# Top-k attention and two MLPs on one core: another cost model for the recorded order, decode's high words in PSUM, and zero products on TensorE

## The chip, the cores and the metric

One core of one Trainium2 chip runs the whole program. The time is the device time of one execution in microseconds, lower is better. Five engines work side by side, each on its own list of instructions: PE (TensorE: products; its weight loads are PEld), DVE (VectorE), ACT (ScalarE), POOL (GpSimd) and SP, which here issues almost all DMA transfers, those that transpose among them. TensorE's clock is granted at one of two levels, 1.2 and 2.4 GHz.

## The reference

Attention keeps the 32 largest scores of each row, and its output goes through two MLPs, which the kernel treats as 18 tiles of 128 tokens:

```python
scores = scale * np.matmul(q, k.transpose(0, 1, 3, 2))       # batch 4, 8 heads, 576 x 576, head size 64
kth = np.partition(scores, -top_k, axis=-1)[..., -top_k:-top_k + 1]
scores = np.where(scores >= kth, scores, -1000000000.0)
attn = softmax(scores)                                         # written out in the reference
x = attn @ v                                                   # as 2304 x 512
h = x @ w_in;  g = where(h >= 1, h, where(h <= -1, 0, (h + 1) ** 2 / 4));  x = g @ w_out     # 512 -> 2048 -> 512
h = max(x @ w_in2, 0);  out = (h * h) @ w_out2
```

## The kernel before

**The work.** 144 slots of attention (18 token tiles T of 8 heads) each take four products into the PSUM tile `both` on PE (`scores`; eight half-height ones in the two tiles that straddle a batch), four MAX8 and three MATCH_REPLACE8 on DVE (`topk_ops`, names `m8`, `W`), three passes on ACT with small ones on POOL between them (`nb` is the bias that `exp_bias` makes), a high and a low half `pc` of the probabilities in 16 bits, a DMA transpose `pT`, and 14 products into `acc` (`attend`). The MLPs run as 144 groups, each a quarter of one tile in one MLP: twelve products into an `h` tile of PSUM (`mlp_in`, from `T_x` or `T_y`, which are transposed activations), the activation on ACT and DVE, high and low halves `g` on ACT and POOL, a DMA transpose `gT`, and twelve products into `o` (`mlp_out`). All products of the MLPs are of 512 columns.

**The weights.** The four matrices come as 64-bit floats in two 32-bit words. For a chunk, `w_decode` (L496) lets ACT shape the high words in place (in `wall`, in SBUF), POOL shape the low words into the chunk's place, and DVE join the two with one SCALAR_TENSOR_TENSOR. There are 62 whole chunks and four half ones. `w_norm` adds four small products of each whole chunk to a running sum of its matrix, the PSUM tile `gram`; from the finished sum comes a scale (through a product named `all_`), and `w_split` (L569) makes high and low 16-bit halves of each chunk, some of them through a PSUM tile `lo_`.

**PSUM.** The ring `ps_h` has two buffers, which serve the `h` tiles, the `lo_` tiles and the `all_` products in turn. `gram` and `o` have two buffers of their own in `ps_o`.

**The order.** Nothing is issued while the program is written down. The class `Book` records each operation (`note`, L194), gives it a cost by hand-written rules (`costs`, L261), and `order` (L291) plays a list scheduler through them: on each engine the ready operation with the smallest key goes first, keys being steps of a plan, and the planned starts set the order in which `emit` (L382) hands everything to the engines. Each engine then works through its own list strictly in that order and waits by semaphores for what it really needs. A transfer is planned to land 0.3 us after its share of the wire (L356). The planner takes DVE and POOL as independent.

Of the kernel before, what the change touches and what calls it, by code (L numbers as in the profile page):

```python
# [7 lines left out]
F16 = mybir.dt.float16  # L8
F32 = mybir.dt.float32
I32 = mybir.dt.int32  # L10
U16 = mybir.dt.uint16
BF16 = mybir.dt.bfloat16
AF = mybir.ActivationFunctionType
ALU = mybir.AluOpType
AX = mybir.AxisListType

P = 128
# [28 lines left out]
    half=((15, 150, 158), (14, 161, 168)), wn=1, ws_i1=45, ws_o1=80, ws_i2=113, ws_o2=183, sp_i1=55, sp_o1=87,  # L46
# [13 lines left out]
class View:  # L60


    __slots__ = ("tile", "ap", "how")
# [78 lines left out]


class Op:
    __slots__ = ("n", "engine", "fn", "args", "kwargs", "deps", "succ", "tiles", "new", "cost", "key", "ready", "start", "missing", "load", "move", "banks")


class Book:
# [36 lines left out]
    def note(self, engine, method, fn, args, kwargs):  # L185
        op = Op()
# [18 lines left out]
        for v in ins:  # L205
            c = v.cover()
# [4 lines left out]
        for v in outs:  # L211
            c = v.cover()
            t = v.tile
# [30 lines left out]
        deps.discard(op.n)  # L244
        op.deps = deps
        op.banks = set()
        for v in views:
            if v.tile.ring.psum and v.tile.name in ("both", "acc"):
                c = v.cover()
                op.banks.update((v.tile.name, b) for b in range(c[2] // 2048, (c[3] - 1) // 2048 + 1))  # L250
# [45 lines left out]
    def order(self):  # L296
# [9 lines left out]
        free = dict.fromkeys(engines, 0.0)  # L306
# [2 lines left out]
        now = {e: [] for e in engines}  # L309
        wire = 0.0  # L310
        out = []
        banks = {}

        def ask(op):
            while op.new:
# [13 lines left out]
        while len(out) < len(ops):  # L329
            best = None  # L330
            for e in engines:
                if now[e]:
                    t = free[e]
                elif soon[e]:
                    t = max(free[e], soon[e][0][0])
# [6 lines left out]
            t, e = best  # L342
            while soon[e] and soon[e][0][0] <= t:
                op = ops[heapq.heappop(soon[e])[1]]
                heapq.heappush(now[e], (op.key, op.n))
            op = ops[heapq.heappop(now[e])[1]]
# [3 lines left out]
                continue  # L350
            op.start = t
            busy, took = op.cost
            free[e] = t + busy
            if e == "SP":
                wire = max(wire, t + 1.6) + took
                end = wire + 0.3  # L356
            else:
                end = t + took
            for b in op.banks:
# [42 lines left out]
def tile_topk_attention_mlp_mlp(  # L402
# [42 lines left out]
    ident = cpool.tile([P, P], BF16, tag="ident", name="ident")  # L445
    ones = cpool.tile([P, P], BF16, tag="ones", name="ones")
    neg = cpool.tile([P, P], F16, tag="neg", name="neg")

    def square_norm(src, acc, junk):
        ACT.activation(junk, src, AF.Square, accum_out=acc)  # L450
# [65 lines left out]
    def w_decode(name, c, *half):  # L516
        d = wall[:, W[name]["at"] + c + 1, :].bitcast(I32)
        if half:
            d = d[:, 256 * half[0] : 256 * half[0] + 256]
        words = lambda: raw[(name, c, *half)].rearrange("p (n w) -> p n w", w=2)  # L520
        halves = lambda: raw[(name, c, *half)].bitcast(U16).rearrange("p (n w) -> p n w", w=4)
        hi = lambda: words()[:, :, 1]


        low = lambda: halves()[:, :, 1]
        return [
            lambda: ACT.activation(hi(), hi(), AF.Prelu, scale=2.0**-112, alpha=-(2.0**32)),
            lambda: POOL.tensor_scalar(d, low(), 2.0**-13, 2.0**-14 - 0.5, op0=ALU.mult, op1=ALU.add),
            lambda: DVE.scalar_tensor_tensor(d, hi().bitcast(I32), 3, d, op0=ALU.logical_shift_left, op1=ALU.bitwise_or),
        ]  # L530

    gram = {}
# [17 lines left out]
    def make_ident():  # L550
        t = wall[:, 0, 0:P].bitcast(I32)
        POOL.iota(t, pattern=[[1, P]], base=0, channel_multiplier=-1)
        POOL.memset(ones, 1.0)
        DVE.tensor_scalar(ident, t, 0.0, None, op0=ALU.is_equal)
        DVE.tensor_scalar(neg, ident, -1.0, None, op0=ALU.mult)

# [9 lines left out]
        return diags[name, at]  # L566


    def w_split(name, c):  # L569
        src = wall[:, W[name]["at"] + c + 1, :]  # L570
        hi, lo = w_hi(name, c, 0, 512), w_lo(name, c, 0, 512)
        s = W[name]["s"]
# [504 lines left out]
    def mlp_in(n, fb):  # L1077
        m, T, j = group(n)
        w = "i1" if m == 1 else "i2"
        src = xT[T] if m == 1 else yT[T]  # L1080
        if fb == 0:
            hps[n] = ps_h.tile([P, 4, P], F32, tag="h", name=f"h_{n}")
        h = hps[n].rearrange("p a b -> p (a b)")
        c = 4 * j + fb
        PE.matmul(h, src[:, 0, fb, :], w_hi(w, c, 0, 512), start=(fb == 0), stop=False)
        PE.matmul(h, src[:, 0, fb, :], w_lo(w, c, 0, 512), start=False, stop=False)
        PE.matmul(h, src[:, 1, fb, :], w_hi(w, c, 0, 512), start=False, stop=(fb == 3))

# [241 lines left out]
    first = {}  # L1330
# [93 lines left out]
```

## Time and profile before

| | us |
|---|---|
| median of 3 runs (lowest, highest) | 1129.77 (1126.63, 1132.04) |
| the profiled execution | 1128.01 |
| its span, first to last instruction | 1126.2 |
| PE busy / DVE busy / ACT busy / POOL busy in the span | 989.6 / 910.6 / 865.6 / 718.5 |

The span is the profiled execution without 1.8 us that lie around it. Every time below is of that one execution. Nearly all instructions are recorded by one line, so rows are told apart by tile and shape. "Idle" is the time that an engine stood still just before an instruction, with what released it. PEclk is the mean granted TensorE clock of a stretch as a share of 2.4 GHz; its records begin at 71 us, and before that the column shows 1.00.

### The profile page before, as it was taken

Reading aid. Unit: us, or ns where it says so; the run is one execution under the profiler, and the core shown is the slowest. Engines: PE = TensorE matmul, PEld = TensorE weight load, DVE = VectorE, ACT = ScalarE, POOL = GpSimd, SP = SyncE. Lnnn points to the kernel's source line nnn. Section 1 sums busy time; section 2 is a strip of 40 time slices with the busy share of each in tenths; the row PEclk is TensorE's granted clock in tenths of the full one; section 3 lists DMA queues with packets and bytes.
Section 4 is the critical chain, followed back from the end, with each engine's and each line's share of the span. In section 5 each row is a group of like instructions: output and inputs, shape, how many; then the busy total and the mean of one; then the engine's idle time right before and its main releaser. Section 6 shows DMA issues by size and latency. Waiting matters only on the chain.

```text
span 1126.2 us, 20691 instructions
## 1 busy us (share of the span) xinstructions
PE 989.6 (88%) x6676; PEld 482.4 (43%) x6676; DVE 910.6 (81%) x1967; ACT 865.6 (77%) x1605; POOL 718.5 (64%) x1182
## 2 busy tenths in 40 slices
PE   1257667689998989999999999999999999999997
PEld 1133333334444434444444544444444444444443
DVE  5988887788898887999899989999899999981100
ACT  4769788999867776888789888988778887776542
POOL 4696889989675645566786746567775656453221
PEclk9999788889999999999999999999999999999999
DMA  8987997686895656778987676879767676665332
GB/s 227 319 270 171 269 213 175 135 163 121 166 168 121 114 112 108 150 128 160 157 167 147 121 129 122 156 130 182 152 126 130 114 132 115 112 109 87 67 64 56
DMA packets 463389, 165.22 MB, mean 147 GB/s; under 512 B 441776, under 2 KB 448944, under 8 KB 463280
## 3 DMA queue, kind: packets, MB, share of 16 engines
q1 hardware_dynamic: 459856, 163.05, 71.5%
q10 hardware_dynamic: 3424, 0.85, 0.5%
q8 instruction: 52, 0.85, 0.3%
q14 instruction: 57, 0.47, 0.1%
HBM read 55.31 MB, written 4.72 MB: 53 GB/s over the span
## 4 chain that ended last, share of the span: by engine, by line
PE 38%; DMA 7%; issue 5%; POOL 5%; DVE 5%; ACT 4%; SPq 0%; POOLq 0%; ACTq 0%; DVEq 0%
PE o L385 17%; PE h L385 16%; DMA gT<-g 4%; PE both L385 3%; DVE m L385 2%; PE acc L385 2%; DVE W L385 2%; POOL pc L385 2%; POOL g L385 2%; ACT W L385 1%; DMA T_x<-hl_x 1%; DMA qT<-qhl 1%; ACT r L385 1%; POOL nb L385 1%; DVE r L385 1%
## 5 line engine op out<-in xcount | busy, mean ns | idle before, releaser
L385 PE MATMUL o<-wall,gT 128*128 128x512 f16 x1728 | 430.1, 387 | 19.4 <-DMA gT<-g 19.3
L385 DVE MAX8 m<-W 128x8 f32<-128x576 f32 x432 | 324.3, 755 | 7.1
L385 POOL TENSOR_TENSOR g<-r,g 128x512 f16<-128x512 f32 x144 | 167.6, 1164 | 165.0 <-ACT g L385 145.1
L385 POOL TENSOR_TENSOR pc<-W,pc 128x64 f16<-128x64 f32 (+1 forms) x288 | 207.2, 741 | 102.8 <-ACT pc L385 95.9
L385 PEld LDWEIGHTS <-gT 128*128 128x128 f16 x1728 | 167.3, 99 | 228.4 <-DMA gT<-g 30.1
L385 DVE MATCH_REPLACE8 W<-m,W 128x576 f32<-128x576 f32 x288 | 213.6, 742 | 0.0
L385 PE MATMUL h<-wall,T_x 128*128 128x512 f16 x864 | 208.8, 382 | 4.2 <-DVE r L385 2.1
L385 PE MATMUL h<-wall,T_y 128*128 128x512 f16 x864 | 209.6, 379 | 1.9 <-ACT r L385 1.8
L385 ACT ACTIVATE W<-both,nb 128x576 f32<-128x576 f32 x144 | 106.5, 740 | 86.1 <-POOL nb L385 43.0
L385 DVE MAX8 m<-both 128x8 f32<-128x576 f32 x144 | 108.7, 757 | 48.0 <-PE both L385 40.3
L385 ACT ACTIVATE W<-W,nb,esc 128x576 f32<-128x576 f32 x144 | 124.5, 864 | 8.5 <-POOL nb L385 4.4
L385 PEld LDWEIGHTS <-T_x 128*128 128x128 f16 x864 | 81.2, 98 | 100.4 <-issue 10.0
L385 PEld LDWEIGHTS <-T_y 128*128 128x128 f16 x864 | 80.9, 98 | 92.3 <-ACT r L385 1.7
L385 PE MATMUL both<-kst,qT 128*128 128x64 f16 (+3 forms) x640 | 101.8, 300 | 20.8 <-ACT W L385 20.1
L385 PEld LDWEIGHTS <-pT 128*128 128x128 f16 (+1 forms) x2240 | 92.7, 103 | 55.8 <-issue 24.7
L385 DVE MATCH_REPLACE8 W<-m,both 128x576 f32<-128x576 f32 x144 | 107.5, 747 | 0.0
L385 PE MATMUL acc<-vst,pT 128*128 128x65 f16 (+1 forms) x2240 | 101.1, 197 | 5.7 <-DVE x L385 3.3
L385 ACT ACTIVATE g<-r 128x512 f16<-128x512 f32 x144 | 90.3, 627 | 13.9 <-DVE r L385 12.3
L385 ACT ACTIVATE pc<-W 128x576 f16<-128x576 f32 x144 | 97.7, 679 | 1.5
L385 ACT ACTIVATE r<-r 128x512 f32<-128x512 f32 x144 | 90.4, 628 | 2.0
L385 DVE SCALAR_TENSOR_TENSOR r<-h,G,r 128x512 f32<-128x512 f32 x72 | 53.2, 739 | 36.4 <-ACT h L385 33.7
L385 ACT ACTIVATE r<-h 128x512 f32<-128x512 f32 x72 | 42.5, 590 | 51.9 <-PE h L385 50.5
(143 smaller groups left out, 1102.8 us busy)
## 6 DMA issues: line engine op xcount, KB each, us to landing
wall<-in_moe_w_in_dram SPq DMA_DIRECT2D x32, 512.0 KB, 7.8
wall<-in_moe_w_out_dram SPq DMA_DIRECT2D x30, 512.0 KB, 6.2
out_dram<-ob SPq DMA_DIRECT2D x18, 256.0 KB, 2.3
l_q<-in_q_dram SPq DMA_DIRECT2D x16, 256.0 KB, 3.5
n_v<-in_v_dram SPq DMA_DIRECT2D x24, 144.0 KB, 2.9
n_k<-in_k_dram SPq DMA_DIRECT2D x12, 288.0 KB, 3.2
l_k<-in_k_dram SPq DMA_DIRECT2D x12, 288.0 KB, 3.4
pT<-pc SPq DMA_TRANSPOSE x144, 3.4
```

Source lines behind the costliest of these rows:

```text
L385: op.fn(*(real(a) for a in op.args), **{k: real(a) for k, a in op.kwargs.items()})
```

## The change

1. **The planner's costs.** An operation of DVE with two inputs in SBUF of more than 64 elements (`port`) and any operation of POOL are planned as excluding each other. The landing of a transposing transfer is planned 1.6 us later than before (`LATE`).
2. **The decode.** POOL's step comes first; ACT writes the high words into a fresh tile `hi_` of the ring `ps_h` instead of in place; DVE reads them from there, so that it has one input in SBUF. In the planner (`hold`) ACT's step follows POOL's.
3. **The first product of an `h` tile** is planned after the split of the four chunks of weights that the tile needs.
4. **Zero products.** `warm` looks at the finished plan of PE. Where a product is planned to start more than 0.9 us after the one before it (0.6 us of margin, `SPARE`, and 0.3), it puts in products of a zero matrix `none`, which add zero to the sum that was opened last and is still open: as many of 128 columns (into `gram`) or of 512 (elsewhere) as fill the planned gap up to the margin. POOL sets `none` once.

```diff
@@ note @@
+        op.port = engine == "DVE" and method in ("scalar_tensor_tensor", "tensor_tensor") and sum(isinstance(v, View) and not v.tile.ring.psum and v.elements() > 64 for v in args[1:]) > 1
@@ order @@
             busy, took = op.cost
+            if e == "POOL" and port > t:
+                busy, took = busy + port - t, took + port - t
+            elif op.port:
+                late = max(free["POOL"] - t, 0.0)
+                busy, took = busy + late, took + late
+                port = t + busy
             free[e] = t + busy
             if e == "SP":
                 wire = max(wire, t + 1.6) + took
-                end = wire + 0.3
+                end = wire + (0.3 if op.load else 0.3 + LATE)
...
-        return sorted(out, key=lambda op: (op.start, op.n))
+        return sorted(out + self.warm(out), key=lambda op: (op.start, op.n))
+
+    def warm(self, out):
+        extra, open_, last = [], {}, None
+        for op in sorted((op for op in out if op.engine == "PE"), key=lambda op: (op.start, op.n)):
+            if last is not None:
+                t, end = last.start + last.cost[0] + 0.02, op.start - SPARE
+                tile = next(reversed(open_), None)
+                while tile is not None and end - t > 0.3:
+                    n = min(tile.shape[-1] * (4 if len(tile.shape) == 3 else 1), 512) if tile.name[:4] != "gram" else P
+                    v = open_[tile]
...
+                    f.args, f.kwargs = (v, self.idle[1], rhs), dict(start=False, stop=False)
+                    f.deps, f.tiles, f.new, f.start, f.cost = {last.n}, [tile], [], t, (n / 2375, n / 2375 + 0.165)
+                    extra.append(f)
+                    t += n / 2375
...
+SPARE = 0.6
+LATE = 1.6
@@ w_decode @@
+        def top():
+            t = ps_h.tile([P, 4, P], F32, tag="h", name=f"hi_{name}_{c}").rearrange("p a b -> p (a b)")
+            high.append(t[:, 0:256] if half else t)
+            book.hold = (high.pop(0),)
+            ACT.activation(high[0], hi(), AF.Prelu, scale=2.0**-112, alpha=-(2.0**32))
+            book.hold = ()
...
         return [
-            lambda: ACT.activation(hi(), hi(), AF.Prelu, scale=2.0**-112, alpha=-(2.0**32)),
-            lambda: POOL.tensor_scalar(d, low(), 2.0**-13, 2.0**-14 - 0.5, op0=ALU.mult, op1=ALU.add),
-            lambda: DVE.scalar_tensor_tensor(d, hi().bitcast(I32), 3, d, op0=ALU.logical_shift_left, op1=ALU.bitwise_or),
+            bottom,
+            top,
+            lambda: DVE.scalar_tensor_tensor(d, high[0].bitcast(I32), 3, d, op0=ALU.logical_shift_left, op1=ALU.bitwise_or),
         ]
@@ mlp_in @@
         if fb == 0:
             hps[n] = ps_h.tile([P, 4, P], F32, tag="h", name=f"h_{n}")
+            book.hold = tuple(split_at[w, 4 * j + i] for i in range(4))
```

**What stands where now.** PE has 740 zero products beside the 6652 that it had: 689 of 128 columns in `gram` sums and 51 of 512 columns (48 into `o` tiles, 3 into `lo_` tiles). 370 of them stand ahead of `all_i1`, the product that follows the first matrix's sum, 336 between it and `all_o2`, the last of these, and 34 behind that. Ahead of `all_o2` stood 84 products into `h`, 48 into `o` and the scores of 24 slots; now 132, 87 and 29. The numbers in names are of buffers and differ between the kernels.

On PE in the middle of the program, where group 56 (tile 7 of the first MLP) has its twelve products into `o`. Before:

```order
L385 LDWEIGHTS T_x7_6385
L385 MATMUL h_58_6643<-wall_78,T_x7_6385 128x512
L385 LDWEIGHTS pT_69_6572
L385 MATMUL acc_467<-vst_1_5_3721,pT_69_6572 128x65
...
L385 LDWEIGHTS gT_56_6610
L385 MATMUL o_1_7_6679<-wall_78,gT_56_6610 128x512
```

Changed:

```order
L417 LDWEIGHTS pT_69_7372
L417 MATMUL acc_898<-vst_1_5_4515,pT_69_7372 128x65
L417 LDWEIGHTS T_x7_7022
L417 MATMUL h_59_7494<-wall_78,T_x7_7022 128x512
...
L417 LDWEIGHTS T_x7_7022
L417 MATMUL h_59_7494<-wall_78,T_x7_7022 128x512
L417 LDWEIGHTS gT_56_7438
L417 MATMUL o_1_7_7518<-wall_78,gT_56_7438 128x512
```

Before, the twelve products of `h_58` and seven of `acc` stood straight ahead of the first use of `gT_56`; now `h_58` and fourteen of `acc` are further ahead, and eight products of the next group's `h_59` have been put between.

On PE in the stretch in which the last matrix is decoded, ahead of the third group of the first tile (`gT_2`; `gram_o2` is the last matrix's running sum). Before:

```order
L385 LDWEIGHTS pT_15_1676
L385 MATMUL acc_467<-vst_0_7_330,pT_15_1676 128x65
L385 LDWEIGHTS wall_78
L385 MATMUL gram_o2_1428<-wall_78 128x128
...
L385 LDWEIGHTS gT_2_1736
L385 MATMUL o_1_0_1589<-wall_78,gT_2_1736 128x512
```

Changed:

```order
L417 LDWEIGHTS pT_16_2323
L417 MATMUL acc_898<-vst_0_0_88,pT_16_2323 128x65
L417 LDWEIGHTS none_84
L417 MATMUL gram_o2_2103<-neg_91,none_84 128x128
...
L417 LDWEIGHTS gT_2_2390
L417 MATMUL o_1_0_2154<-wall_78,gT_2_2390 128x512
```

Four real products of `gram_o2` stood there; now 38 zero products (`none`) do, and no real one.

On DVE in slot 12, with the decode's joining steps between the steps of the top-k. Before:

```order
L385 MATCH_REPLACE W_12_1192<-m8_12_1138,both_183 128x576
L385 SCALAR_TENSOR_TENSOR wall_78<-wall_78 128x512
L385 MAX m8_12_1138<-W_12_1192 128x8
L385 SCALAR_TENSOR_TENSOR wall_78<-wall_78 128x512
L385 MATCH_REPLACE W_12_1192<-m8_12_1138,W_12_1192 128x576
```

Changed:

```order
L417 MATCH_REPLACE W_12_1595<-m8_12_1564,both_173 128x576
L417 SCALAR_TENSOR_TENSOR wall_78<-hi_i2_3_1593,wall_78 128x512
L417 MAX m8_12_1564<-W_12_1595 128x8
L417 MATCH_REPLACE W_12_1595<-m8_12_1564,W_12_1595 128x576
L417 SCALAR_TENSOR_TENSOR wall_78<-hi_i2_4_1617,wall_78 128x512
```

The joining steps stand as densely as before among MAX and MATCH_REPLACE; what moved is their first input, from `wall` to a `hi_` tile, so that the ring `ps_h` takes 66 more tiles in the course of the decode.

## Rows read from the trace of the kernel before

**Rows 1.** Page, block 1: busy time, share of the span, instructions by engine.

```profile
PE 989.6 (88%) x6676; PEld 482.4 (43%) x6676; DVE 910.6 (81%) x1967; ACT 865.6 (77%) x1605; POOL 718.5 (64%) x1182
```

**Rows 2.** By stretch, its length: PE, PEld, DVE, ACT, POOL busy, PEclk, DMA, GB/s.

```profile
0.00:72.00 72.00, 20.94 (x139) 11.78 (x139) 54.38 (x119) 42.74 (x81) 45.05 (x86) 1.00 0.98 289
72.00:160.00 88.00, 60.42 (x409) 31.25 (x409) 76.95 (x164) 74.82 (x140) 71.35 (x96) 0.86 0.80 216
160.00:232.00 72.00, 48.97 (x317) 23.57 (x316) 55.92 (x123) 63.82 (x134) 66.31 (x87) 0.81 0.76 159
232.00:400.00 168.00, 155.03 (x1117) 74.21 (x1116) 148.50 (x350) 134.48 (x260) 122.39 (x207) 0.96 0.75 140
400.00:1010.00 610.00, 596.23 (x4151) 292.51 (x4148) 560.28 (x1182) 496.39 (x900) 384.39 (x677) 1.00 0.74 135
1010.00:1126.20 116.20, 107.97 (x551) 49.10 (x549) 14.55 (x32) 53.33 (x92) 29.01 (x34) 0.98 0.37 69
```

**Rows 3.** PE's timeline, 175 to 191 us; start, us, what, [idle before, releaser].

```profile
175.22 2.75 PE L385 MATMUL h<-wall,T_x 128*128 128x512 f16 x12
...
179.22 0.41 PE L385 MATMUL gram_o<-wall 128*128 128x128 bf16 x4 [0.59 <-DVE wall L385]
...
184.81 0.61 PE L385 MATMUL gram_o<-wall 128*128 128x128 bf16 x4 [2.43 <-DVE wall L385]
185.22 5.32 PE L385 MATMUL o<-wall,gT 128*128 128x512 f16 x12
```

**Rows 4.** Waits, 72 to 232 us: total us, times, longest.

```profile
PE gram_o L385 <- DVE wall L385: 15.8, 10, 4.0
DVE wall L385 <- POOL wall L385: 7.4, 12, 1.2
DVE m L385 <- PE both L385: 6.5, 5, 3.2
```

**Rows 5.** PE's waits, 232 us to the end.

```profile
PE o L385 <- DMA gT<-g: 15.2, 17, 2.4
PE both L385 <- ACT W L385: 4.3, 3, 2.7
```

**Rows 6.** PE's timeline around one such wait, and at the end.

```profile
562.16 0.38 PE L385 MATMUL acc<-vst,pT 128*128 128x65 f16 x7
563.60 2.76 PE L385 MATMUL o<-wall,gT 128*128 128x512 f16 x12 [1.05 <-DMA gT<-g]
...
1112.94 2.76 PE L385 MATMUL o<-wall,gT 128*128 128x512 f16 x12 [0.60 <-DMA gT<-g]
1118.11 4.25 PE L385 MATMUL o<-wall,gT 128*128 128x512 f16 x12 [2.40 <-DMA gT<-g]
```

**Rows 7.** `wall` on DVE and POOL: ns min/median/max, first and last start.

```profile
L385 DVE SCALAR_TENSOR_TENSOR wall<-wall x62: 666/692/1534, 10.6 to 206.5; 128x512 int32<-128x512 int32 x62
...
L385 POOL TENSOR_SCALAR wall<-wall x62: 638/653/1227, 10.0 to 205.4; 128x512 int32<-128x512 uint16 x62
```

**Rows 8.** Groups by shape: busy, mean ns, idle before.

```profile
L385 DVE SCALAR_TENSOR_TENSOR r<-h,G,r 128x512 f32<-128x512 f32 x72 | 53.2, 739 | 36.4 <-ACT h L385 33.7 <-POOL g L385 2.4 <-POOL pc L385 0.3
L385 DVE SCALAR_TENSOR_TENSOR wall<-wall 128x512 int32<-128x512 int32 x62 | 50.3, 816 | 21.1 <-POOL wall L385 10.3 <-ACT wall L385 9.7 <-POOL nb L385 0.8
L385 POOL TENSOR_SCALAR wall<-wall 128x512 int32<-128x512 uint16 x62 | 47.2, 761 | 15.9 <-DMA wall<-in_moe_w_in_dram 9.2 <-PE lo_i L385 1.8
L385 ACT ACTIVATE wall<-wall 128x512 f32<-128x512 f32 x62 | 40.1, 667 | 10.9 <-DMA wall<-in_moe_w_in_dram 6.3 <-issue 4.5
```

**Rows 9.** PE's first and last `all_` product of the weights: when.

```profile
65.59 0.27 PE L385 MATMUL all_i<-dg_i,ones 128*128 128x128 bf16 x1 [0.38 <-DVE dg_i L385]
...
226.70 0.27 PE L385 MATMUL all_o<-dg_o,ones 128*128 128x128 bf16 x1 [1.76 <-DVE r L385]
```

**Rows 10.** Tile `gram_o` on PE: ns min/median/max.

```profile
L385 PE MATMUL gram_o<-wall x128: 217/220/314, 68.0 to 224.6; 128*128 128x128 bf16 x128
```

More of the change, by code (lines that the diff above doesn't have):

```diff
@@ L144 @@
 class Op:
-    __slots__ = ("n", "engine", "fn", "args", "kwargs", "deps", "succ", "tiles", "new", "cost", "key", "ready", "start", "missing", "load", "move", "banks")
+    __slots__ = ("n", "engine", "fn", "args", "kwargs", "deps", "succ", "tiles", "new", "cost", "key", "ready", "start", "missing", "load", "move", "banks", "port")
 class Book:
@@ L311, in order @@
         out = []
-        banks = {}
+        banks, port = {}, 0.0
         def ask(op):
@@ L379, in order @@
         self.length = max(free.values())
-        return sorted(out, key=lambda op: (op.start, op.n))
+        return sorted(out + self.warm(out), key=lambda op: (op.start, op.n))
[8 more added lines that the diff above has]
+                    v = open_[tile]
+                    f = Op()
+                    f.n, f.engine, f.fn, f.move, f.load, f.port, f.banks = len(self.ops) + len(extra), "PE", self.idle[0], "matmul", False, False, set()
+                    rhs = self.idle[2] if n == P else self.idle[2].unsqueeze(1).to_broadcast([P, 4, P])
+                    f.args, f.kwargs = (v, self.idle[1], rhs), dict(start=False, stop=False)
+                    f.deps, f.tiles, f.new, f.start, f.cost = {last.n}, [tile], [], t, (n / 2375, n / 2375 + 0.165)
+                    extra.append(f)
+                    t += n / 2375
+            tile = op.args[0].tile
+            if op.kwargs["stop"]:
+                open_.pop(tile, None)
+            elif tile.name not in ("acc", "both"):
+                open_.pop(tile, None)
+                open_[tile] = op.args[0]
+            last = op
+        return extra
     def emit(self, ops):
@@ L447, in tile_topk_attention_mlp_mlp @@
     neg = cpool.tile([P, P], F16, tag="neg", name="neg")
+    none = cpool.tile([P, P], F16, tag="none", name="none")
+    book.idle = (nc.tensor.matmul, none, neg)
     def square_norm(src, acc, junk):
@@ L525, in w_decode, with bottom @@
         low = lambda: halves()[:, :, 1]
+        high = []
+        def top():
[4 more added lines that the diff above has]
+            book.hold = ()
+        def bottom():
+            POOL.tensor_scalar(d, low(), 2.0**-13, 2.0**-14 - 0.5, op0=ALU.mult, op1=ALU.add)
+            high.append(len(book.ops) - 1)
         return [
-            lambda: ACT.activation(hi(), hi(), AF.Prelu, scale=2.0**-112, alpha=-(2.0**32)),
-            lambda: POOL.tensor_scalar(d, low(), 2.0**-13, 2.0**-14 - 0.5, op0=ALU.mult, op1=ALU.add),
-            lambda: DVE.scalar_tensor_tensor(d, hi().bitcast(I32), 3, d, op0=ALU.logical_shift_left, op1=ALU.bitwise_or),
+            bottom,
+            top,
+            lambda: DVE.scalar_tensor_tensor(d, high[0].bitcast(I32), 3, d, op0=ALU.logical_shift_left, op1=ALU.bitwise_or),
         ]
@@ L553, in make_ident @@
         POOL.memset(ones, 1.0)
+        POOL.memset(none, 0.0)
         DVE.tensor_scalar(ident, t, 0.0, None, op0=ALU.is_equal)
@@ L566, in w_diag, with last, w_split_ops @@
         return diags[name, at]
+    split_at = {}
     def w_split(name, c):
+        first, high, low = w_split_ops(name, c)
+        def last():
+            low()
+            split_at[name, c] = len(book.ops) - 1
+        return [first, high, last]
+    def w_split_ops(name, c):
         src = wall[:, W[name]["at"] + c + 1, :]
@@ L1085, in mlp_in @@
         PE.matmul(h, src[:, 0, fb, :], w_hi(w, c, 0, 512), start=(fb == 0), stop=False)
+        book.hold = ()
         PE.matmul(h, src[:, 0, fb, :], w_lo(w, c, 0, 512), start=False, stop=False)
```

## The prediction

> **What bounds the kernel now.** I first read the busy shares [rows 1]: PE is busy for 989.6 us of a span of 1126.2, DVE for 910.6, and no engine is full over the whole. The stretches [rows 2] show three phases. From 0 to 72 us the weights arrive and PE is busy for 20.9 us. From 72 to 232 us, while the weights are decoded and the first slots run, PE is busy for 60.4 + 49.0 = 109.4 of 160 us, DVE for 132.9, ACT for 138.6, POOL for 137.7: three engines at 83 to 87%, none full, and each waits for the others in turn [rows 4]. From 232 us on PE is the bound: 155.0 of 168 us, then 596.2 of 610, then 108.0 of 116.2. DVE has done nearly all its work by 1010 us, and the last 116 us are PE's alone. So the end comes sooner in two ways: PE idles less after 232 us (35.0 us of idle in 894), or the phase before it reaches the same point earlier.
>
> The second thing to see is the clock. PEclk is 0.86, 0.81 and 0.96 in the three stretches from 72 to 400 us [rows 2]. With levels of 1.2 and 2.4 GHz these means are 24.6, 27.4 and 13.4 us at the lower one (twice the missing share times the length). Twelve products of 512 columns take 5.32 us there, after PE had stood still for 2.43 us, against 2.75 us at the higher level [rows 3]. The last twelve products of the program take 4.25 us instead of 2.76, after a wait of 2.40 us [rows 6].
>
> **The parts.** *Later transposes.* After 232 us PE stood idle 17 times, 15.2 us in all, for `gT` just before products into `o` [rows 5]; one of the waits, 1.05 us at 563 us, is the place in the order shown above [rows 6]. There eight `h` products now stand between, 8 x 0.216 = 1.7 us of work ((2.76 - 0.38) / 11 = 0.216 us a product [rows 6]). The last two waits (0.60 and 2.40 us) have nothing to go ahead of them, which leaves 12.2 us in 15 waits. If each is covered, 12 us come back; if the work put between is then missed elsewhere, nothing does. I take 9, nearer to the full cover, because the covering product group is ready work in the row that I could compare. What is late next is `both`, which waited 4.3 us in that stretch for ACT to read the scores before [rows 5].
>
> *The clock.* In the three stretches PE was busy for 69, 68 and 92% of the time, so about 17 + 19 + 12 = 48 us of its busy time lie at 1.2 GHz, and half, 24 us, would go if the clock never fell. That is the upper bound. From 232 to 400 us PE is the bound and 6 us count fully if the clock holds there, but few zero products stand behind 227 us (34, all told); I take 4. From 72 to 232 us the shorter products (18 us less) only help those who wait for PE, and DVE's wait for `both` there is 6.5 us [rows 4]; I take 4. The last twelve products can save 1.5 us (4.25 - 2.76), but 17 zero products of 0.216 us, 3.7 us, stand in waits of 0.60 + 2.40 us, so 0.7 us is lost again; I take 1. Together 9, with 2 and 20 as ends.
>
> *High words in PSUM.* The joining step on DVE takes 692 ns at the median, 816 in the mean and up to 1534 [rows 7, 8]; POOL's step takes 653, 761 and 1227. Both tails are long, as if the two engines held each other up. The nearest row of a joining step that reads PSUM is `r<-h,G,r` with 739 ns [rows 8]. So DVE gains 62 x (816 - 739) = 4.8 us and POOL 62 x (761 - 653) = 6.7 us. The Trainium skill (SBUF — State Buffer, Who interferes with whom) gives the cause: a DVE instruction with two inputs in SBUF and a GpSimd instruction that reads SBUF exclude each other, and the later one waits. By that rule alone each joining step would fall to its median, 62 x (816 - 692) = 7.7 us; the PSUM row says that 2.9 us of that go to the slower source. Neither engine is full there, so of 11.5 us I take 3, with 0 and 10 as ends. The planner's exclusion moves the remaining clashes apart; it is in these 10.
>
> *The ring `ps_h`.* Each high word holds a buffer through ACT's step and DVE's, 0.67 + 0.74 us [rows 8], and about 0.6 between and after, by an estimate from DVE's 12 waits of 7.4 us for POOL [rows 4]: 2 us, 62 times. An `h` group behind it waits at worst for one such hold. About seven groups (84 `h` products stand ahead of `all_o2`, which came at 226.7 us [rows 9]) start in this phase, 14 us at worst. At best nothing is lost, since PE idles 51 us there anyway. I count 2, near the best, because products in that stretch mostly wait for DVE [rows 4].
>
> *The zero products.* Four `gram` products take 0.41 us, a single one at least 0.217 [rows 3, 10]: (0.41 - 0.217) / 3 = 0.064 us each at 2.4 GHz. At 1.2 GHz it is (0.61 - 0.31) / 3 = 0.100. The 370 ahead of `all_i1` (65.6 us [rows 9]) lie where PE idles for 51 of 72 us. The 336 up to `all_o2` (226.7 us) cost 319 x 0.064 + 17 x 0.216 = 24 us, in about 50 us of idle. The 34 behind cost 7.3 us. Hidden, they cost nothing; I count 2 for overruns, with 14 as the bad end.
>
> **Sum:** 9 + 9 + 3 - 2 - 2 = 17 us off 1128.0 us, 1111. That execution is 1.8 us below the median of the runs; I say 1112.
>
> **The rivals.** *A: the front does not move.* ACT and POOL with 87 and 86% of 72 to 232 us stay the pace, the clock and the exclusion save time that nobody waits for, and only the covered waits and the tail count: 1128 - 9 - 1 = 1118. For it: DVE waited for PE only 6.5 us there [rows 4]. Against it: DVE and POOL, which gain from the PSUM source, are two of the three busy ones.
>
> *B: the waits move.* The 12 us of `gT` return as waits for `both`, `T_x` or `acc`, because PE's work between was needed later: 1128 - 3 = 1125, no change that can be told. For it: less than half of PE's 35 us of idle after 232 us is for `gT`, so there are other waits to take its place. Against it: the products put forward are ready.
>
> *C: the zero products get in the way (slower).* PE's list is strict, so a zero product that is not needed delays what stands behind. If the clock in 72 to 232 us stays at its present 0.84 or below, runs of up to 51 zero products take 0.100 us each instead of the planned 0.054 and outlast their margin. Overrun: 319 x 0.046 + 17 x 0.21 = 18 us at worst, and the 34 later ones 7 us where PE has no idle time. With the clock's gain gone, 1128 + 25 - 9 - 3 = 1141. It decides once overruns exceed the other gains, about 12 us. For it: planned gaps are longer than real ones wherever a landing is now planned 1.6 us too late; `gram` products also precede `both`, and DVE waits for `both`. Against it: many of the zero products have idle time around them, and they keep PE working.
>
> *D: the front shrinks by much more.* DVE's 27 us of idle in 72 to 232 us are mostly waits for engines that themselves are delayed by one another; if half of that closes, `gT` is covered in full and the clock gives 8: 1128 - 13 - 12 - 8 = 1095.
>
> **Chances.** The forecast, 1104 to 1117: 0.37. A: 0.22. B: 0.14. C: 0.13. D: 0.14. The range that leaves out no more than 2 in 10 is 1094 to 1134: it holds the forecast, A, B, most of D and the mild part of C. A measurement of this kernel can tell about 0.5%, 5.6 us. Faster by more than that: forecast, A, D, 0.73. Within it: B and a little of C, 0.15. Slower: 0.12.
>
> **What would show it.** Right, if PEclk from 72 to 400 us is above 0.93, PE's wait of `o` for `gT` after 232 us falls below 6 us, the joining step's mean falls to about 740 ns, and the last scores come 10 us or so earlier than 1010 us. The front was wrong if DVE's and ACT's busy shares from 72 to 232 us stay at 83 and 87%, and PE becomes 92% busy no earlier than at 232 us. Wrong altogether, if DVE's wait for `both` grows while PE runs zero products, or if `hi_` tiles make ACT or PE wait for the ring.

## The result, and the profile after

| | before | after |
|---|---|---|
| median, us (lowest, highest) | 1129.24 (1126.63, 1132.04) | 1113.89 (1109.44, 1115.43) |
| the profiled execution, us | 1128.01 | 1109.44 |
| its span, us | 1126.2 | 1107.6 |

The ratio is 0.9854, with a 95% interval of 0.9822 to 0.9887: faster by 15.4 us, against 17 in the prediction's sum. The forecast time was 1112 with a range of 1094 to 1134. The profiled execution is the fastest of the four, 4.5 us below their median, which has to be kept in mind wherever spans are compared below. Any kernel's execution now and then comes out far longer: seven such ones of the experiments below (one of e4, one of b4, two of e7, three of the kernel before; 1158 to 6033 us) are left out of all medians, and as b4's profile is of one of them, no rows of b4 are read.

The page's busy times, as in [rows 1]:

```profile
PE 1018.1 (92%) x7416; PEld 519.5 (47%) x7416; DVE 905.7 (82%) x1967; ACT 859.5 (78%) x1605; POOL 693.5 (63%) x1183
```

POOL has lost 25.0 us of busy time (718.5 to 693.5), though it executes the same work and one instruction more. DVE has lost 4.9. PE has gained 28.5, with 740 more products. The stretches, with the columns of [rows 2]:

```profile
0.00:72.00 72.00, 41.52 (x554) 35.92 (x554) 55.51 (x127) 43.60 (x82) 42.46 (x94) 0.93 0.97 296
72.00:160.00 88.00, 67.35 (x568) 36.20 (x568) 80.08 (x182) 82.08 (x160) 62.33 (x101) 1.00 0.92 224
160.00:232.00 72.00, 59.10 (x544) 34.60 (x544) 60.46 (x124) 66.24 (x139) 58.83 (x87) 1.00 0.84 185
232.00:400.00 168.00, 152.35 (x1095) 72.53 (x1094) 143.79 (x332) 133.93 (x254) 120.98 (x199) 0.97 0.72 130
400.00:1010.00 610.00, 603.94 (x4217) 297.67 (x4215) 559.00 (x1189) 494.00 (x906) 386.70 (x681) 1.00 0.76 136
1010.00:1107.60 97.60, 93.81 (x447) 42.57 (x445) 6.84 (x17) 39.68 (x69) 22.22 (x24) 1.00 0.34 65
```

The granted clock is 1.00, 1.00 and 0.97 from 72 to 400 us, where it was 0.86, 0.81 and 0.96. POOL is busy for 62.33 + 58.83 = 121.2 us from 72 to 232 us (137.7 before), DVE for 140.5 (132.9), ACT for 148.3 (138.6): POOL has dropped out of the three that paced this phase, and the two others do more in the same time. PE's waits, to set beside [rows 4, 5], first for 72 to 232 us and then from 232 us on:

```profile
PE both L417 <- ACT W L417: 8.2, 9, 1.6
PE gram_o L417 <- DVE wall L417: 8.0, 11, 1.8
```

```profile
PE both L417 <- DVE W L417: 4.8, 6, 1.2
PE both L417 <- ACT W L417: 4.0, 4, 1.6
PE all_v L417 <- DVE sc_v L417: 2.9, 1, 2.9
PE o L417 <- POOL wall L417: 2.8, 4, 0.8
```

The waits of `o` for `gT` no longer stand among the longer ones. New ones are there instead: for `both`, and for the split of the last matrix. The decode steps by tile (ns min/median/max, first and last start), as in [rows 7], and below them ACT's step by shape with its mean:

```profile
L417 DVE SCALAR_TENSOR_TENSOR wall<-hi_o,wall x34: 406/680/692, 63.2 to 232.4; 128x512 int32<-128x512 int32 x30, 128x256 int32<-128x256 int32 x4
L417 DVE SCALAR_TENSOR_TENSOR wall<-hi_i,wall x32: 662/682/692, 16.8 to 147.1; 128x512 int32<-128x512 int32 x32
```

```profile
L417 POOL TENSOR_SCALAR wall<-wall x62: 637/658/1017, 10.3 to 208.0; 128x512 int32<-128x512 uint16 x62
```

```profile
L417 ACT ACTIVATE hi_i<-wall 128x512 f32<-128x512 f32 x32 | 20.1, 630 | 11.1 <-DMA wall<-in_moe_w_in_dram 6.1 <-issue 4.6 <-DVE wall L417 0.5
```

The joining step's long tail is gone: at most 692 ns where it was 1534, 683 in the mean where it was 816. ACT's step into PSUM takes 630 where the one in place took 667. The last matrix's `all_` product, however, comes later than the 226.70 us of [rows 9], and the last scores earlier than the 1010 us that the prediction names (tiles on PE, first and last start):

```profile
L417 PE MATMUL all_o<-dg_o,ones x2: 216/217/218, 108.3 to 240.6; 128*128 128x128 bf16 x2
```

```profile
L417 PE MATMUL both<-kst,qT x640: 189/317/631, 18.1 to 994.0; 128*128 128x64 f16 x122, 128*64 128x64 f16 x17, 128*64 128x512 f16 x15, 128*128 128x512 f16 x6
```

**Where the time went.** The columns of all of PE's products, without the zero ones and at 2.4 GHz, come to 914.6 us in each of these kernels (the 48 products of 32-bit floats count twice; they take 0.70 to 0.75 us in the kernel before, others of 512 columns some 0.4). The table says when so much of that sum had been started (the products of the profiled execution summed in order of time; "last" is the start of the last product). The kernels named e and b are the experiments below.

| work started, us | before | after | e1 | e2 | e3 | b1 | b2 | b3 |
|---|---|---|---|---|---|---|---|---|
| 120 | 271.9 | 254.0 | 262.7 | 256.7 | 273.3 | 271.4 | 276.2 | 262.3 |
| 150 | 304.6 | 302.6 | 312.8 | 291.9 | 303.4 | 307.0 | 308.6 | 299.6 |
| 250 | 424.7 | 410.7 | 421.0 | 399.2 | 419.2 | 428.1 | 421.1 | 412.2 |
| last | 1121.7 | 1103.4 | 1116.4 | 1093.4 | 1116.7 | 1124.4 | 1128.0 | 1105.8 |
| from 250 to last | 697.0 | 692.7 | 695.4 | 694.2 | 697.5 | 696.3 | 706.9 | 693.6 |

Of the 18.3 us that the profiled execution gains, 14.0 lie ahead of the mark of 250. At the mark of 120 the lead is even 17.9, and at 150 only 2.0: between the two PE loses nearly all of it again, and has most of it back by 250. The loss is a stall that the kernel before does not have. PE's timeline there (columns as in [rows 3]):

```profile
251.09 0.38 PE L417 MATMUL o<-wall,gT 128*128 128x512 f16 x1 [0.29 <-ACT wall L417]
251.31 0.59 PE L417 MATMUL o<-neg,none 128*128 128x512 f16 x2
252.66 0.59 PE L417 MATMUL o<-wall,gT 128*128 128x512 f16 x2 [0.77 <-POOL wall L417]
...
255.16 1.06 PE L417 MATMUL o<-wall,gT 128*128 128x512 f16 x3 [0.80 <-POOL wall L417]
256.78 0.65 PE L417 MATMUL both<-kst,qT 128*128 128x64 f16 x4 [0.56 <-ACT W L417]
258.22 1.47 PE L417 MATMUL o<-wall,gT 128*128 128x512 f16 x3 [0.79 <-POOL wall L417]
```

Every few products into `o` wait for chunks of the last matrix whose split is not done; its sum was complete only at 240.6 us. From 250 to 305 us PE is busy for 44.0 us here and for 50.5 in the kernel before, and the granted clock is 0.91 there against 0.97. The waits of `o` for `wall` make 4.2 us of the missing time. Two waits are of like size, `all_v` for DVE (4.0 us) and `h` for `sc_y` (1.9), so the late split is a part of the stall and not all of it. What each part of the change has to do with this is what the experiments were for.

### The profile page after: what moved, and what is told of

It reads as the page before. It is cut to its first block, busy times and chain, and to the rows that moved or that the text cites. A ratio compares the mean times of both kernels' runs of the same rounds, so it can differ in the third digit from the quotient of the medians.

```text
span 1107.6 us, 22192 instructions
## 1 busy us (share of the span) xinstructions
PE 1018.1 (92%) x7416; PEld 519.5 (47%) x7416; DVE 905.7 (82%) x1967; ACT 859.5 (78%) x1605; POOL 693.5 (63%) x1183
## 4 chain that ended last, share of the span: by engine, by line
PE 54%; DVE 12%; ACT 10%; POOL 7%; issue 5%; DMA 3%; SPq 0%; DVEq 0%; ACTq 0%; POOLq 0%
PE o L417 25%; PE h L417 22%; DVE m L417 5%; DVE W L417 5%; PE both L417 4%; PE acc L417 4%; POOL wall L417 3%; ACT W L417 3%; POOL pc L417 1%; ACT wall L417 1%; ACT r L417 1%; DMA n_v<-in_v_dram 1%; POOL g L417 1%; ACT pc L417 1%; DVE r L417 1%
## 5 line engine op out<-in xcount | busy, mean ns | idle before, releaser
L417 PE MATMUL o<-wall,gT 128*128 128x512 f16 x1728 | 412.9, 381 | 4.7 <-POOL wall L417 2.8
L417 PE MATMUL acc<-vst,pT 128*128 128x65 f16 (+1 forms) x2240 | 98.6, 195 | 0.9 <-DVE x L417 0.5
```

Source lines behind the costliest of these rows:

```text
L417: op.fn(*(real(a) for a in op.args), **{k: real(a) for k, a in op.kwargs.items()})
```

## The experiments

Times are medians; the kernel before, run beside each, had medians of 1128.06 to 1129.68, so that they can be set side by side. The changed kernel was run four times only, and the interval of its ratio is 7 us wide, so a difference from its 1113.89 us is good to 3 or 4 us.

| kernel | edit | us | ratio [95%] |
|---|---|---|---|
| e1 | after without zero products | 1123.19 | 0.9945 [0.9925, 0.9965] |
| e2 | after without the later landing | 1098.17 | 0.9735 [0.9714, 0.9756] |
| e3 | after with the old decode steps | 1123.52 | 0.9946 [0.9927, 0.9965] |
| e4 | after without the planner's exclusion | 1117.40 | 0.9907 [0.9884, 0.9929] |
| b1 | before with zero products | 1128.04 | 0.9992 [0.9974, 1.0011] |
| b2 | before with the later landing | 1130.68 | 1.0024 [1.0005, 1.0043] |
| b3 | before with high words in PSUM | 1111.74 | 0.9850 [0.9825, 0.9875] |
| b4 | b3 with zero products | 1108.81 | 0.9824 [0.9798, 0.9850] |
| b5 | b3, most high words in SBUF again | 1123.80 | 0.9954 [0.9934, 0.9974] |
| e5 | after, weights ahead in the plan | 1111.45 | 0.9845 [0.9820, 0.9870] |
| e6 | e2, weights ahead in the plan | 1103.16 | 0.9776 [0.9754, 0.9799] |
| e7 | e2 with half the margin of the zero products | 1102.99 | 0.9776 [0.9749, 0.9804] |

### One part taken out

**e1: no zero products.**

```diff
-        return sorted(out + self.warm(out), key=lambda op: (op.start, op.n))
+        return sorted(out, key=lambda op: (op.start, op.n))
```

> The changed kernel without its 740 zero products, everything else the same. Theory 1 (the terms of the sum): the clock's 9 us go and 2 us of overruns come back, 7 us slower than the changed kernel, PEclk from 72 to 232 us back near 0.84. Theory 2 (the front's lead is lost again between 255 and 300 us, where the last matrix's split is waited for, and the transposes carry the net): the first 250 us get slower by some 10 us, but the end by under 3 us.

It took 1123.19 us, so the zero products are worth 9.3 us in the changed kernel. They are put into a finished plan, so the order of everything else is the same. Its stretches:

```profile
72.00:160.00 88.00, 60.62 (x435) 29.96 (x435) 76.75 (x174) 79.05 (x154) 59.18 (x97) 0.96 0.89 212
160.00:232.00 72.00, 51.03 (x327) 25.20 (x325) 57.94 (x121) 63.76 (x134) 58.24 (x83) 0.81 0.85 179
232.00:400.00 168.00, 150.47 (x1060) 71.27 (x1059) 139.24 (x324) 130.08 (x249) 119.56 (x199) 0.94 0.66 127
```

Without zero products PEclk is 0.96, 0.81 and 0.94 in place of 1.00, 1.00 and 0.97, and at the mark of 120 this kernel is 8.7 us behind the changed one. So they hold the clock, and here that is worth time.

**e2: no later landing.**

```diff
-LATE = 1.6
+LATE = 0.0
```

> The changed kernel with the planned landing of transposes back at the old value. Theory 1: PE's waits of o for gT after 232 us, now none, come back with 10 to 15 us, and the time rises by 9 us. Theory 2: they come back too, and the time rises by 12 to 16 us, nearly the whole gain. Rival B (waits only move): the time changes by under 3 us.

It took 1098.17 us, 15.7 less than the changed kernel (13.4 by the ratios), where all three cases of the expectation had it slower or the same: the later landing costs time here, and without it the kernel is the fastest of all that were run. Two of its stretches, its last `all_` product, and PE's longest waits from 232 us on:

```profile
160.00:232.00 72.00, 61.53 (x563) 37.32 (x562) 58.82 (x123) 66.57 (x141) 58.83 (x84) 0.95 0.81 183
232.00:400.00 168.00, 159.60 (x1156) 76.72 (x1155) 153.55 (x354) 141.77 (x268) 127.56 (x215) 1.00 0.76 142
```

```profile
L417 PE MATMUL all_o<-dg_o,ones x2: 217/218/219, 111.0 to 231.2; 128*128 128x128 bf16 x2
```

```profile
PE o L417 <- DMA gT<-g: 9.9, 12, 1.7
...
PE both L417 <- ACT W L417: 1.7, 3, 1.0
```

The waits for `gT` are back, 9.9 us in 12 places. But PE is busy for 159.60 us from 232 to 400 us, where the changed kernel has 152.35: the stall is gone, and the last matrix's sum is complete at 231.2 us instead of 240.6. From the mark of 250 on the two need 694.2 and 692.7 us, so the later landing gives some 1.5 us in the long part for which it was made, and costs 11.5 ahead of it (410.7 against 399.2). The profiled executions are 10.0 us apart and the medians 15.7, since the changed kernel's profiled one is its fastest and that of e2 is 1.3 us above its median.

The margin delays the last matrix's sum only together with the high words in PSUM. With the old decode steps the last `all_` product comes at 228.9 us (b2) and 227.0 us (e3) with the later landing, and at 226.7 us in the kernel before. With the high words in PSUM it comes at 230.9 to 234.9 us without the later landing (e2, e6, e7, b3) and at 237.1 to 249.5 us with it (the changed kernel, e1, e4, e5).

**e3: the old decode steps**, in place in SBUF, with the rest of the change.

```diff
-            bottom,
-            top,
-            lambda: DVE.scalar_tensor_tensor(d, high[0].bitcast(I32), 3, d, ...),
+            lambda: ACT.activation(hi(), hi(), AF.Prelu, ...),
+            lambda: POOL.tensor_scalar(d, low(), ...),
+            lambda: DVE.scalar_tensor_tensor(d, hi().bitcast(I32), 3, d, ...),
```

> The changed kernel with the old decode: ACT writes the high words in place in SBUF, DVE reads both inputs from SBUF; the planner still keeps such steps and POOL apart. Theory 1: 2 to 3 us slower, the joining step's mean back above 0.72 us. If keeping them apart in the plan does all the work, the step's mean stays near 0.69 us but DVE and POOL wait more, and the time rises by over 5 us. If the ring costs more than the source gains: faster by 2 us or more.

It took 1123.52 us: the way through PSUM is worth 9.6 us in the changed kernel, where the first case of the expectation had 2 to 3. The plan is another one, too, with 1072 zero products. The joining step and POOL's step by shape (busy, mean ns, idle before):

```profile
L417 DVE SCALAR_TENSOR_TENSOR wall<-wall 128x512 int32<-128x512 int32 x62 | 51.4, 837 | 9.5 <-POOL wall L417 6.8 <-ACT wall L417 2.2 <-issue 0.2
...
L417 POOL TENSOR_SCALAR wall<-wall 128x512 int32<-128x512 uint16 x62 | 45.4, 732 | 15.7 <-DMA wall<-in_moe_w_in_dram 11.3
```

837 and 732 ns, where the changed kernel has 683 and 669. The planner's exclusion was in force in this kernel, and it did not keep the two engines apart on the chip. The last `all_` product came at 227.0 us, 13.6 earlier than in the changed kernel; so the time is lost although the last matrix is ready sooner.

**e4: no exclusion in the planner.** The two conditions on `port` are switched off.

```diff
-        op.port = engine == "DVE" and ...
+        op.port = False and engine == "DVE" and ...
...
-            if e == "POOL" and port > t:
+            if False and e == "POOL" and port > t:
```

> The changed kernel without the planner's exclusion of DVE's two-input steps and POOL. With the high words in PSUM few such steps are left (five in the decode phase, 18 elsewhere), so theory 1 and 2 both expect under 3 us either way; what it shows beyond that is how far the time moves when the order changes for no cause of weight.

It took 1117.40 us, 3.5 more by the medians and 6.0 by the ratios. No real work is removed by this edit (the zero products become 801), so 4 to 6 us is also about what another order of the same work can do, and smaller differences between kernels of different orders are not to be read as the worth of a part.

### One part alone

**b1: before, with zero products** (`warm`, 838 of them).

> The kernel before with zero products alone (838 in its own planned gaps). If the clock is worth what taking the zero products from the changed kernel showed (9 us), this gains 7 to 10 us. If they need the other order, it gains under 3 us, or loses where real work comes before its planned start.

It took 1128.04 us, no change. Two stretches:

```profile
72.00:160.00 88.00, 67.27 (x576) 40.26 (x575) 74.19 (x163) 73.00 (x135) 71.63 (x94) 0.89 0.80 211
160.00:232.00 72.00, 55.17 (x482) 31.93 (x481) 58.25 (x126) 65.58 (x140) 66.99 (x90) 0.92 0.80 172
```

The clock rose from 0.86 and 0.81 to 0.89 and 0.92, and PE's faster products bought nothing: POOL is busy for 71.63 + 66.99 = 138.6 us there, as it was in the kernel before (137.7), DVE for 132.4 (132.9).

**b2: before, with the later landing.**

```diff
-                end = wire + 0.3
+                end = wire + (0.3 if op.load else 0.3 + LATE)
...
+LATE = 1.6
```

> The kernel before with the later planned landing alone. The prediction's term: PE's waits of o for gT after 232 us (15.2 us) mostly go and the time falls by 9 us. Rival B (the waits move): they go, waits for both, acc or h take their place, and the time changes by under 4 us either way.

It took 1130.68 us, no gain and if anything slower (2.0 us). PE's waits from 232 us on:

```profile
PE both L385 <- ACT W L385: 15.5, 11, 3.2
PE acc L385 <- ACT vst L385: 3.5, 3, 1.6
PE o L385 <- DMA gT<-g: 3.2, 3, 2.4
```

`o` waits 3.2 us for `gT`, in place of 15.2 [rows 5]; `both` waits 15.5 us for ACT to be done with the scores before, in place of 4.3. Twelve us of wait left one line of the list and eleven came back on another, and from the mark of 250 on this kernel is the slowest of all in the table, by 9 us (its profiled execution is 3.3 us above its median).

**b3: before, with the high words in PSUM** and POOL's step first; no exclusion, no later landing, no zero products.

```diff
         return [
-            lambda: ACT.activation(hi(), hi(), AF.Prelu, ...),
-            lambda: POOL.tensor_scalar(d, low(), ...),
-            lambda: DVE.scalar_tensor_tensor(d, hi().bitcast(I32), 3, d, ...),
+            bottom,
+            top,
+            lambda: DVE.scalar_tensor_tensor(d, high[0].bitcast(I32), 3, d, ...),
         ]
```

> The kernel before with the decode's high words in PSUM alone (POOL's step planned first, as in the change). The prediction's term: 1 to 5 us faster. What the reverse experiment showed (the old decode in the changed kernel costs 9.6 us): 7 to 11 us faster, with POOL's step near 0.66 us and the joining step near 0.68 us. If the ring is what counts: slower.

It took 1111.74 us: this part alone gives 17 us, as much as the whole change and more than either case of the expectation (1 to 5, 7 to 11). Its busy times and two stretches:

```profile
PE 984.7 (89%) x6676; PEld 478.6 (43%) x6676; DVE 907.2 (82%) x1967; ACT 864.7 (78%) x1605; POOL 694.7 (63%) x1182
```

```profile
72.00:160.00 88.00, 64.77 (x451) 31.97 (x452) 77.53 (x179) 79.97 (x154) 60.84 (x100) 0.91 0.87 215
160.00:232.00 72.00, 52.33 (x340) 25.05 (x339) 57.04 (x117) 64.59 (x136) 57.42 (x82) 0.83 0.83 175
```

POOL's busy time falls by 23.8 us, to 694.7. The clock from 72 to 232 us is little better than before, and in b1 a higher clock alone brought nothing, so the gain is not the clock's. Of the 15.9 us by which the last product starts earlier (1105.8 against 1121.7), 12.5 are there at the mark of 250, though the last `all_` product comes at 234.9 us, 8.2 later than before.

**b4: b3 with zero products** (669).

> The kernel before with the high words in PSUM and zero products (669), without later landings, the planner's exclusion and the rule for h. If zero products are worth 9 us once the front is not held by DVE and POOL, as in the changed kernel: about 1103 us. If they only made up for what the later landings broke there: 1109 to 1113, as with the high words alone.

It took 1108.81 us, 2.9 less than b3, with intervals that overlap. The zero products are thus worth 0.7 us in the kernel before, some 3 beside the PSUM source, and 9.3 in the changed kernel, which has the exclusion, the rule on the first product of `h` and the later landing as well. No run takes that rule alone, so how much of the difference is its doing stays open.

**b5: b3 with most of the high words in SBUF again**, though still in a tile of their own, so that the decode keeps its new sequence of steps. 48 of the 62 whole chunks use it.

```diff
-            t = ps_h.tile([P, 4, P], F32, tag="h", ...)
+            if half or name == "o2":
+                t = ps_h.tile([P, 4, P], F32, tag="h", ...)
+            else:
+                t = pool.tile([P, S], F32, tag=("kl", "khl")[c % 2], ...)[:, 0:512]
```

> As the kernel before with the high words in PSUM alone, but 48 of the 62 whole chunks (all but the last matrix's) get their high words in a fresh SBUF tile of two alternating buffers instead: the raw words' buffer comes free as early, the joining step has two SBUF inputs again. If the clash of DVE and POOL is what cost the time, 48/62 of the 17 us are lost: about 1124 us, with the joining step's mean above 0.78 us for these. If the early release or the other order of steps is what counts: 1110 to 1114 us.

It took 1123.80 us, 12.1 more than b3. The joining steps of the first and third matrix, those of the two others (14 of the 30 read PSUM), and POOL's step:

```profile
L385 POOL TENSOR_SCALAR wall<-wall 128x512 int32<-128x512 uint16 x62 | 45.3, 730 | 12.0 <-DVE m L385 4.8 <-DMA wall<-in_moe_w_in_dram 2.3 <-DMA wall<-in_moe_w_out_dram 0.2
...
L385 DVE SCALAR_TENSOR_TENSOR wall<-hi_i,wall 128x512 int32<-128x512 int32 x32 | 28.3, 893 | 7.8 <-ACT hi_i L385 6.7 <-issue 0.9
...
L385 DVE SCALAR_TENSOR_TENSOR wall<-hi_o,wall 128x512 int32<-128x512 int32 x30 | 23.4, 787 | 8.4 <-ACT hi_o L385 4.0 <-POOL pc L385 3.3 <-POOL wall L385 0.9
```

893 ns with the source in SBUF, 681 in b3 with the source in PSUM, and POOL's step is back from 661 to 730. Neither the new sequence nor the separate tile makes the steps short; the place of the source does. That a DVE instruction with two inputs in SBUF and a GpSimd instruction that reads SBUF shut each other out is what the Trainium skill states (SBUF — State Buffer, Who interferes with whom). This pair of runs agrees: 893 and 730 ns against 681 and 661. Of the 12.1 us a part may have another cause: the tiles of this run share two buffers (`kl`, `khl`) with the raw words of the half chunks, and the last `all_` product comes at 249.8 us, against 234.9 in b3. No run separates the two.

### Attempts to take the stall away

**e5: the weights ahead.** In the planner's keys the steps of decode and split are moved forward by 8.

```diff
-    soon={'s': 8, 'att': 8, 'a': 8, 'x': 24},
+    soon={'split': 8, 'dec': 8, 's': 8, 'att': 8, 'a': 8, 'x': 24},
```

> The changed kernel with decode and split of the weights put ahead in the planner's keys (8 steps of the plan sooner), so that the last join stands two slots earlier. If the stall between 255 and 300 us is the wait for the last matrix's split, which came late because the last join did, the finished sum comes before 235 us instead of at 240.6, the stall shrinks, and the time falls by 6 to 12 us. If something else holds PE there, the time stays within 3 us.

It took 1111.45 us, 2.4 less than the changed kernel and within what an order alone can do. The last `all_` product came at 237.1 us, only 3.5 earlier. Yet the waits of `o` for chunks are gone from its trace (behind 232 us `o` has one wait on its list, 0.4 us for `gT`), and PE is busy for 49.7 us from 250 to 305 us. The work that those waits had held up gained nothing: the mark of 120 comes at 270.4 us, 16 later than in the changed kernel, and those of 150 and 250 at 302.7 and 410.0, within 1 us of it. So the waits for the split, in which the stall showed, did not set the time, as the second case of the expectation had it. What did is open, and the run does not tell by which way the later landing delays the last chunks.

**e6: the same in e2.**

> The changed kernel with landings planned as before (which gave 1098 us) and decode and split of the weights put 8 steps ahead in the planner's keys (which gave 2 us in the changed kernel). If the last matrix's split is still waited for: 1090 to 1095 us. If not: 1096 to 1102 us, or slower where the keys hold up the top-k.

It took 1103.16 us, 5.0 more than e2 and outside both ranges of the expectation, which had named a slower kernel as possible where the keys hold up the top-k. Whether that is the cause was not shown; 5.0 us is also what another order can do (e4).

**e7: e2 with a smaller margin** for the zero products, and so with more of them.

```diff
-SPARE = 0.6
+SPARE = 0.3
```

> The changed kernel with landings planned as before and a margin of 0.3 instead of 0.6 us ahead of the next product, so that gaps are filled further and smaller gaps too. If the clock still falls in gaps left open: 1 to 4 us faster than 1098 us. If zero products stand in the way of real ones that come early: 1 to 5 us slower.

It took 1102.99 us, 4.8 more than e2, as the second case of the expectation had it. The real work has the order of e2 here, and there are 974 zero products in place of 745, so the 4.8 us are the price of the additional ones. At the mark of 250 the two kernels are still within 0.7 us (399.9 and 399.2); from there to the last product e7 needs 697.7 us and e2 694.2, so nearly all of it is lost in the long part.

## Why the prediction was right, and where it was not

The total was right, 1112 against 1113.9, but measured alone two terms of the sum were wrong by more than 10 us each, in opposite directions (b3: 17 for 3; b2: 2 lost for 9 gained). That the total came out is luck. Step by step:

**High words in PSUM: 3 predicted, 17 alone (b3), 9.6 when taken out (e3).** The mechanism was the one that [rows 7, 8] suggested; the size was off. The step that failed is "Neither engine is full there, so of 11.5 us I take 3". Three engines at 83 to 87%, each waiting for the others in turn, can be a bound together, where what one of them saves, the next gets earlier; that reading is argued, the 12.5 us that b3 has gained at the mark of 250 are measured. And 11.5 us was too small a base. It counted the two steps that clash, but POOL lost 25.0 us, because other steps of POOL in this phase were long as well. One of its small steps for the scores, before and after (by shape: busy, mean ns, idle before):

```profile
L385 POOL TENSOR_SCALAR nb<-m,esc 128x1 f32<-128x1 f32 x144 | 57.3, 398 | 1.0
```

```profile
L417 POOL TENSOR_SCALAR nb<-m,esc 128x1 f32<-128x1 f32 x144 | 53.5, 372 | 0.8
```

144 steps on one column each became 26 ns shorter in the mean, 3.8 us together. The gain lies where the joining steps are: ahead of 235 us all steps into `nb` took 434 ns in the mean (46 of them) and now take 281 (52), behind it 275 and 278. The weights' step gave 5.7 us (47.2 to 41.5), and other groups the rest. The price of the source was wrong, too: the 739 ns of `r<-h,G,r` [rows 8] was taken for what a read from PSUM costs, and the joining step takes 683 from PSUM. The nearest row was one of the same shape but of another type and other operands; the median of the step itself, 692 [rows 7], was nearer.

**Later transposes: 9 predicted; 2 lost alone (b2), 13 to 16 lost in the changed kernel (e2).** The waits for `gT` went as said, below 6 us. The step that failed is that I took 9 "because the covering product group is ready work in the row that I could compare". Ready work put ahead is not free when PE is busy for 96% of the time, as from 232 us on in the kernel before: what stood behind it is late, and that was `both`, which the prediction itself had named as "what is late next". So rival B's mechanism was the true one for this part where it stood alone. Neither the sum nor a rival had foreseen that beside the high words in PSUM the same margin delays the last chunks of weights, by 9.4 us for the last `all_` product, and costs 11.5 us up to the mark of 250 (e2 against after).

**The clock: 9 predicted, 9.3 in the changed kernel (e1), 0.7 in the kernel before (b1).** PEclk is above 0.93 in all the stretches from 72 to 400 us, as the test in the prediction asked. The size was right in one company only, and its split (4 for 232 to 400 us, 4 for 72 to 232, 1 at the end) was not: of the 13.0 us by which e1's last product is later, 8.7 are there at the mark of 120 and 10.3 at 250. The worry that the text had stated, that shorter products help only those who wait for PE, fits b1. It does not explain b4, where the clash is gone and they are worth some 3 us; what makes 9.3 of it in the changed kernel is not shown.

**The ring and the zero products: 2 lost each.** In the changed kernel ACT waits for DVE ahead of `hi_i` for 0.5 us in all (the last cause in the row of ACT's step above) and ahead of `hi_o` for 1.3, so as waits the ring cost about what was said. The order may have cost more. The half chunks of the kernel before are joined from their tile `w_o`, the last at 223.7 us:

```profile
L385 DVE SCALAR_TENSOR_TENSOR wall<-w_o,wall x4: 416/425/426, 213.7 to 223.7; 128x256 int32<-128x256 int32 x4
```

In the changed kernel the last starts at 232.4 us (the row of `hi_o` above). In all kernels read here whose last matrix goes through `ps_h` it starts at 226.7 to 244.9 us, in all with the old decode steps at 223.5 to 224.7; that it is the ring that delays it is not shown. The cost of the zero products is inside the 9.3 us of e1, and rival C did not come: from 72 to 232 us the wait of `gram_o` for DVE fell from 15.8 to 8.0 us, and DVE's wait for `both` from 6.5 to 6.0 (9.3 without zero products, e1).

**The tail: 1 predicted.** PE's timeline at the end, beside [rows 6]:

```profile
1094.79 2.11 PE L417 MATMUL o<-neg,none 128*128 128x512 f16 x9
1096.74 2.75 PE L417 MATMUL o<-wall,gT 128*128 128x512 f16 x12
1099.33 1.89 PE L417 MATMUL o<-neg,none 128*128 128x512 f16 x8
1101.05 2.75 PE L417 MATMUL o<-wall,gT 128*128 128x512 f16 x12
```

Both last groups run in 2.75 us with zero products ahead of them, where the second took 4.25. From the start of the next to last group to the end of the span it is 1107.6 - 1096.74 = 10.9 us, before 1126.2 - 1112.94 = 13.3: 2.4 us gained.

**The rivals.** A (the front does not move) fell: 14.0 of 18.3 us are gained ahead of the mark of 250. D (the front shrinks by much more) is what e2 shows, 1098 against D's 1095, though not through `gT` being covered. The sign of a wrong front, shares of DVE and ACT that stay at 83 and 87%, did not come: they rose to 88 and 93%, while POOL's fell from 86 to 76%. The share of PE that the text wanted beside them tells little, since zero products count as busy. The sum itself has a small slip: 1111 and 1.8 are 1112.8, and the text says 1112.

**What stays open.** The parts do not add up. From b4 to e2 the exclusion and the rule on the first product of `h` bring 10.6 us together, with e4 giving 4 to 6 for the exclusion (in another company), and e4 to e6 show that the order alone moves the time by 2 to 6 us. How much of e2's lead is a lucky order is not settled. That the later landing costs time is shown in the changed kernel; in the kernel before it brings no gain, and its loss of 2.0 us is barely clear of noise. By which way it delays the last chunks, and only beside the high words in PSUM, is not shown.

## What to carry to other kernels

Where several engines stand at 80 to 90% and wait for each other in turn, price a removed clash at the tails of everything that the engines do in that phase, and do not discount it because no engine is full. A planned landing that is later may not remove a wait on a busy engine but choose who waits, as in b2; look at what is next on the list of waits before counting it as gain. Work that holds the clock up was worth 0.7, some 3 and 9.3 us in three companies here, so try it last, on top of the other changes.

## What was not expected of the hardware

A joining step of 128 x 512 with one of its inputs in PSUM took 683 ns, no longer than the one with both in SBUF takes at its median (692), and ACT's pass took 630 ns (`hi_i`) and 636 (`hi_o`) into PSUM against 667 in place. Products of zeros, 689 of 128 columns and 51 of 512, went with a granted clock of 1.00 from 72 to 232 us, where the same order without them had 0.96 and 0.81 (e1).
